# A gated delta rule and a soft mixture of experts on one core: 32-token chunks with the inverse on VectorE, against 64-token chunks with a block inverse on GpSimd and a list-scheduled order

## The chip, the core and the metric

One core of a Trainium2 chip runs the whole program. The number that counts is the device time of one launch in microseconds. PE is the matrix engine, DVE the vector engine, ACT the scalar engine, POOL is GpSimd, SP the queue that issues most transfers. All data are float32.

## What is computed

The first block is a delta rule over 768 tokens for 4 batches x 8 heads, head size 48; the second takes its output as 3072 rows of 384 and sends them through 32 slots of 8 experts.

```python
k_n = k / (norm(k) + 1e-06)
for t in range(S):                       # S = 768, for all 32 (b, h)
    kt, vt, bt = k_n[:, :, t], v[:, :, t], beta[:, :, t, None]
    y[:, :, t] = q[:, :, t] @ state
    v_old = state^T @ kt
    state = state + bt * outer(kt, vt - v_old)
x = y as (3072, 384)
logits = x @ phi                         # 32 slots
d = softmax over rows; slot_input = d.T @ x
slot_out[e] = relu(slot_input[e] @ w1[e]) @ w2[e]    # w1 384x1024, w2 1024x384, 8 experts
out = softmax over slots (logits) @ slot_out
```

The recurrence is worked in chunks. Within a chunk the tokens depend on each other through a unit lower triangular matrix (the products of the chunk's keys, scaled by beta). Its inverse T turns R = V - K S into the updates U; then S += K^T U and Y = Q S + (masked Q K^T) U.

## The kernel before

The token axis is cut into 24 chunks of C = 32. Partitions hold 4 head rows x 32 tokens; the 8 remaining (batch, head half) pairs, U = 8, lie along the free axis. A group is GC = 4 chunks, so there are NG = 6 groups.

- `load` (L80) brings k, q and v in, four transfers of 48 KB a chunk and tensor, in pieces of 192 bytes, from SP (the first q from ACT).
- `prep` transposes K and Q on PE (L173), evicts them on ACT (L176) and forms key-key and query-key products (L188), evicted by ACT into Lc (L194) and masked by DVE into AT (L195).
- `invert` works on one group. DVE transposes Lc in 32x32 blocks (L207), takes norms (L221 to L233), POOL scales the matrix by rows (L230, 128x1024), DVE eliminates in 31 steps of a multiply and a subtract each (L240, L243), POOL scales the result (L247) and DVE transposes it back into TT (L253). POOL also clears the next tt (L211).
- `chunk` is the step of the state: K S and Q S in one loop (L278), R on DVE (L283), T R (L289), U on ACT (L292), K^T U (L299), the state's two halves to SBUF by DVE and ACT (L309, L311), and the output (L316, L318). K S multiplies by a state of 96 columns whose off-diagonal halves are zero.
- `route` turns a group's outputs into logits, a running softmax over rows and the slots' sums (L336 to L418).
- The order is written out by hand. `prep` runs LEAD = 8 chunks ahead, loads AHEAD = 12. Between the parts of `chunk`, `fill()` puts in a share of the steps of `prep`, of a quarter of `invert` and of a quarter of `route`. Each engine executes its instructions in that order.
- After the loop the experts run. Two w1 (1.5 MB each) are loaded early, the other six and all eight w2 after the attention part's buffers are given back (L152, L156). Then `first` (L543 to L557), `second` (L567), and 24 output blocks (L593 to L600), one store each of 192 KB.

Of the kernel before, what the change touches and what calls it, by code (L numbers as in the profile page):

```python
# [1 line left out]

# [6 lines left out]
F32 = mybir.dt.float32  # L9
# [3 lines left out]
PSUM = bass.MemoryType.PSUM  # L13


@with_exitstack
def kernel(
# [11 lines left out]

# [3 lines left out]
    C = 32  # L44
    G = H // 4
    GC = 4
    NG = S // (GC * C)
    NCH = S // C
    U = B * G
    DP = 64  # L50
    GD = G * D
    E, Dm, F = moe_w1.shape
    NSL = moe_phi.shape[1]
    SPE = NSL // E
    NFC = F // P
    NKT = Dm // P
    assert G == 2 and B == 4 and GC * U == C and Dm == H * D and NSL == C

    cpool = ctx.enter_context(tc.tile_pool(name="const", bufs=1))
    wpool = ctx.enter_context(tc.tile_pool(name="wts", bufs=1))  # L60
    small = ctx.enter_context(tc.tile_pool(name="small", bufs=2))
    att = ExitStack()
    ps = att.enter_context(tc.tile_pool(name="ps", bufs=1, space=PSUM))
    io = att.enter_context(tc.tile_pool(name="io", bufs=2))
    wk = att.enter_context(tc.tile_pool(name="wk", bufs=2))
    psp = att.enter_context(tc.tile_pool(name="psp", bufs=1, space=PSUM))

    def pt(shape):
        return ps.tile(shape, F32, name="pt", tag="pt", bufs=2)


    LEAD, AHEAD = 8, 12
    NK, NQ = AHEAD + 1, AHEAD - LEAD + 1
    Ks = [io.tile([P, U, DP], F32, name=f"K{i}", bufs=1) for i in range(NK)]
    Qs = [io.tile([P, U, DP], F32, name=f"Q{i}", bufs=1) for i in range(NQ)]
    Vt = {}

    def load(src, dst, cc, eng):
        for h in range(4):
            eng.dma_start(  # L80
                out=dst[C * h:C * h + C, :, 0:D],
                in_=src.rearrange("b (g h) s d -> h s (b g) d", h=4)[h, cc * C:(cc + 1) * C])

    def load_k(cc, eng=nc.sync):
        load(k, Ks[cc % NK], cc, eng)

    def load_q(cc, eng=nc.sync):
        load(q, Qs[cc % NQ], cc, eng)

    def load_v(cc, eng=nc.sync):  # L90
        Vt[cc] = io.tile([P, U, D], F32, name="V", tag="V", bufs=7)
        load(v, Vt[cc], cc, eng)

    ident = cpool.tile([P, P], F32, name="ident")
    make_identity(nc, ident)
    for i in range(NK):
        nc.vector.memset(Ks[i][:, :, D:DP], 0.0)
        if i < NQ:
            nc.vector.memset(Qs[i][:, :, D:DP], 0.0)
    load_k(0)  # L100
    load_q(0, nc.scalar)
    load_k(1)
    load_q(1, nc.scalar)
    load_k(2)
    load_q(2)
    load_k(3)
    load_q(3)

    bb = cpool.tile([P, NG, C], F32, name="bb")
    for h in range(4):  # L110
        for c in range(GC):
            p0 = C * h + U * c
            nc.gpsimd.dma_start(
                out=bb[p0:p0 + U],
                in_=beta.rearrange("b (g h) (n c t) -> h c (b g) n t", h=4, c=GC, t=C)[h, c])
    phi = cpool.tile([GD, 4, NSL], F32, name="phi")
    for g in range(G):
        nc.gpsimd.dma_start(
            out=phi[g * D:(g + 1) * D],
            in_=moe_phi[g * 4 * D:(g + 1) * 4 * D].rearrange("(h d) s -> d h s", h=4))  # L120


    hm = cpool.tile([P, 4], F32, name="hm")
    nc.gpsimd.memset(hm, 1.0)
    nc.gpsimd.affine_select(out=hm, in_=hm, compare_op=ALU.is_ge, fill=0.0, base=0,
                            pattern=[[-C, 4]], channel_multiplier=1)
    nc.gpsimd.affine_select(out=hm, in_=hm, compare_op=ALU.is_ge, fill=0.0, base=C - 1,
                            pattern=[[C, 4]], channel_multiplier=-1)

    bdm = cpool.tile([P, 4, C], F32, name="bdm")  # L130
    nc.gpsimd.memset(bdm, 1.0)
    nc.gpsimd.affine_select(out=bdm, in_=bdm, compare_op=ALU.is_ge, fill=0.0, base=-1,
                            pattern=[[C, 4], [1, C]], channel_multiplier=-1)
    nc.vector.tensor_tensor(bdm, bdm, hm.unsqueeze(2).broadcast_to([P, 4, C]), op=ALU.mult)
    tri = cpool.tile([P, C], F32, name="tri")
    nc.vector.tensor_reduce(tri, bdm.rearrange("p h t -> p t h"), axis=AX.X, op=ALU.add)

    psS = psp.tile([P, 4, 512], F32, name="psS")
    St = []
    for i in range(2):  # L140
        t = wk.tile([P, 4, B, GD], F32, name=f"S{i}", bufs=1)
        nc.vector.memset(t, 0.0)
        St.append(t)


    NW1 = 2
    w1t, w2t = {}, {}


    def load_w1(e, pool, bufs):  # L150
        w1t[e] = pool.tile([P, NKT, F], F32, name="w1t", tag="w1t", bufs=bufs)
        nc.sync.dma_start(out=w1t[e], in_=moe_w1[e].rearrange("(p k) f -> p k f", k=NKT))  # L152

    def load_w2(e, pool, bufs):
        w2t[e] = pool.tile([P, NFC, Dm], F32, name="w2t", tag="w2t", bufs=bufs)
        nc.sync.dma_start(out=w2t[e], in_=moe_w2[e].rearrange("(p t) d -> p t d", t=NFC))  # L156

    KQ, AT, Lc, TT, nT = {}, {}, {}, {}, {}  # L160

    def prep(cc):

        n, c = divmod(cc, GC)

        def transposes(bh):
            if bh == 0:
                KQ[cc] = wk.tile([P, B, 2, P], F32, name="KQ", tag="KQ", bufs=LEAD + 1)
            tp = pt([P, 2, 2, P])
            for i in range(2):  # L170
                b = 2 * bh + i
                for a, src in enumerate((Ks[cc % NK], Qs[cc % NQ])):
                    nc.tensor.transpose(  # L173
                        tp[:, i, a, :],
                        src[:, b * G:(b + 1) * G, :].rearrange("p g d -> p (g d)"), ident)
            nc.scalar.activation(KQ[cc][:, 2 * bh:2 * bh + 2], tp, ACT.Copy)  # L176

        def products():
            AT[cc] = wk.tile([P, G, B, C], F32, name="AT", tag="AT", bufs=LEAD + 1)
            if c == 0:  # L180
                Lc[n] = wk.tile([P, C, C], F32, name="Lc", tag="Lc")
            pg = [pt([P, B, 2, C]) for _ in range(G)]
            for b in range(B):
                for h in range(4):
                    for g in range(G):
                        r = slice(DP * g, DP * g + D)
                        rh = slice(C * h, C * h + C)
                        nc.tensor.matmul(pg[g][rh, b], lhsT=KQ[cc][r, b, 0, rh],  # L188
                                         rhs=KQ[cc][r, b, :, rh],
                                         start=True, stop=True, skip_group_check=True)  # L190

            by = Lc[n].rearrange("p t (c b g) -> p c g b t", c=GC, b=B)
            for g in range(G):
                nc.scalar.activation(by[:, c, g], pg[g][:, :, 0, :], ACT.Copy)  # L194
                nc.vector.tensor_tensor(AT[cc][:, g], pg[g][:, :, 1, :],  # L195
                                        tri.unsqueeze(1).broadcast_to([P, B, C]), op=ALU.mult)

        return [lambda bh=bh: transposes(bh) for bh in range(2)] + [products]

    def invert(n):  # L200

        st = {}

        def spread():

            lb = st["lb"] = wk.tile([P, C, C], F32, name="lb", tag="lb", bufs=1)
            nc.vector.transpose(lb.rearrange("p t s -> p (t s)"),  # L207
                                Lc.pop(n).rearrange("p t c -> p (t c)"))
            tt = st["tt"] = wk.tile([P, C, C], F32, name="tt", tag="tt")
            ttf = tt.rearrange("p k i -> p (k i)")  # L210
            nc.gpsimd.memset(ttf, 0.0)  # L211
            nc.gpsimd.memset(ttf[:, 0:C * C:C + 1], 1.0)

        def norms():

            ssq = small.tile([P, C], F32, name="ssq", tag="ssq")
            nrm = small.tile([P, C], F32, name="nrm", tag="nrm")
            rn = small.tile([P, C], F32, name="rn", tag="rn")
            gm = st["gm"] = small.tile([P, C], F32, name="gm", tag="gm")
            dg = st["lb"].rearrange("p t s -> p (t s)")[:, 0:C * C:C + 1]  # L220
            nc.vector.tensor_scalar(ssq, dg, 1e-30, None, op0=ALU.max)  # L221
            nc.scalar.activation(nrm, ssq, ACT.Sqrt)
            nc.vector.reciprocal(rn, nrm)
            nc.vector.tensor_tensor(rn, rn, ssq, op=ALU.mult)
            nc.vector.tensor_tensor(nrm, nrm, rn, op=ALU.add)
            nc.vector.tensor_scalar(nrm, nrm, 0.5, 1e-6, op0=ALU.mult, op1=ALU.add)
# [402 lines left out]
```

## Time and profile before

| | us |
|---|---|
| median of 3 runs (lowest, highest) | 487.07 (486.02, 490.53) |
| span of the profiled execution | 489.7 |
| busy PE, DVE, ACT, POOL in it | 334.7, 245.1, 128.9, 63.6 |
| mean granted clock of PE | 0.729 |

Times in the profile's lines are microseconds, means of one instruction nanoseconds. A line names the engine, the line of the kernel, the operation, output and inputs, shapes, and a count. What stands behind `<-` released the instruction.

The timeline shows the same pattern in each group. The scaling by POOL (L230) stands at 142, 208, 273 and 338 us. The chunk loop ends at 424 us; w1 and w2 arrive from 400 to 461 us; the output goes out from 473 us.

### The profile page before, as it was taken

Reading aid. Unit: us, or ns where it says so; the run is one execution under the profiler, and the core shown is the slowest. Engines: PE = TensorE matmul, PEld = TensorE weight load, DVE = VectorE, ACT = ScalarE, POOL = GpSimd, SP = SyncE. Lnnn points to the kernel's source line nnn. Section 1 sums busy time; section 2 is a strip of 40 time slices with the busy share of each in tenths; the row PEclk is TensorE's granted clock in tenths of the full one; section 3 lists DMA queues with packets and bytes.
Section 4 is the critical chain, followed back from the end, with each engine's and each line's share of the span. In section 5 each row is a group of like instructions: output and inputs, shape, how many; then the busy total and the mean of one; then the engine's idle time right before and its main releaser. Section 6 shows DMA issues by size and latency. Waiting matters only on the chain.

```text
span 489.7 us, 20564 instructions
## 1 busy us (share of the span) xinstructions
PE 334.7 (68%) x9387; PEld 248.3 (51%) x9387; DVE 245.1 (50%) x679; ACT 128.9 (26%) x257; POOL 63.6 (13%) x88
## 2 busy tenths in 40 slices
PE   5743374656766758788677776876875865788586
PEld 4532263545645646666466655665664753532133
DVE  4159716972168942379721788325997212210033
ACT  2331122121322422332422233224312222111012
POOL 9210112012020040020210200202301000000000
PEclk9655556665766759755778577599798797799695
DMA  6557742320322213202221110010300029949427
GB/s 114 86 94 195 205 83 51 52 37 18 52 51 39 46 19 52 50 16 40 51 39 33 19 19 13 9 20 5 113 23 1 4 94 367 424 156 434 208 101 287
DMA packets 84759, 45.53 MB, mean 93 GB/s; under 512 B 79392, under 2 KB 82624, under 8 KB 82624
## 3 DMA queue, kind: packets, MB, share of 16 engines
q1 hardware_dynamic: 81920, 43.67, 32.4%
q8 instruction: 74, 1.21, 1.0%
q10 hardware_dynamic: 2176, 0.39, 0.4%
q0 software_dynamic: 576, 0.15, 0.3%
q14 instruction: 13, 0.11, 0.1%
HBM read 39.47 MB, written 4.72 MB: 90 GB/s over the span
## 4 chain that ended last, share of the span: by engine, by line
DVE 27%; issue 25%; PE 19%; SPq 10%; DMA 10%; POOL 5%; ACT 3%; DVEq 0%; POOLq 0%; ACTq 0%
DVE pr L240 9%; SPq L80 9%; DVE tt L243 9%; DMA w2t<-in_moe_w_dram 4%; PE pso L567 3%; DVE S L309 3%; PE psR L278 2%; PE pt L410 2%; DMA w1t<-in_moe_w_dram 2%; PE psY L278 2%; POOL lb L230 2%; DMA Q<-in_q_dram 2%; DVE TT L253 2%; PE ph L543 1%; DMA out_dram<-ob 1%
## 5 line engine op out<-in xcount | busy, mean ns | idle before, releaser
L240 DVE TENSOR_TENSOR pr<-tt,lb 128x31 f32<-128x31 f32 (+15 forms) x186 | 68.0, 365 | 17.7 <-POOL lb L230 12.2
L243 DVE TENSOR_TENSOR tt<-tt,pr 128x31 f32<-128x31 f32 (+15 forms) x186 | 66.3, 357 | 5.7
L289 PE MATMUL psW<-R,TT 32*32 32x48 f32 x1536 | 29.9, 242 | 47.0 <-DVE R L283 45.5
L173 PE MATMUL pt<-ident,K 128*128 128x128 f32 x96 | 36.0, 396 | 24.1 <-DVE AT L195 18.7
L289 PEld LDWEIGHTS psW<-R,TT 32*32 32x32 f32 x1536 | 25.7, 134 | 52.4 <-DVE R L283 49.3
L176 ACT ACTIVATE KQ<-pt 128x512 f32<-128x512 f32 x48 | 27.1, 595 | 73.9 <-PE pt L173 73.5
L278 PE MATMUL psR<-S,KQ 128*32 128x96 f32 x768 | 33.1, 324 | 17.7 <-DVE S L309 17.0
L316 PE MATMUL psY<-U,AT 32*32 32x48 f32 x1536 | 39.0, 256 | 3.2 <-issue 3.1
L195 DVE TENSOR_TENSOR AT<-pt,tri 128x128 f32<-128x128 f32 x48 | 11.9, 288 | 54.6 <-ACT Lc L194 54.4
L188 PE MATMUL pt<-KQ 48*32 48x64 f32 x1536 | 33.5, 246 | 6.2 <-ACT KQ L176 2.6
L309 DVE COPY S<-psS 48x768 f32<-48x768 f32 x23 | 22.1, 961 | 31.1 <-ACT S L311 30.7
L316 PEld LDWEIGHTS psY<-U,AT 32*32 32x32 f32 x1536 | 31.1, 143 | 9.2 <-issue 7.1
L299 PE MATMUL psS<-U,K 32*48 32x48 f32 x1472 | 25.3, 261 | 14.5 <-ACT U L292 11.6
L278 PEld LDWEIGHTS psR<-S,KQ 128*32 128x32 f32 x768 | 23.7, 145 | 22.4 <-DVE S L309 18.9
L188 PEld LDWEIGHTS pt<-KQ 48*32 48x32 f32 x1536 | 25.0, 119 | 16.0 <-ACT KQ L176 9.5
L173 PEld LDWEIGHTS pt<-ident,K 128*128 128x128 f32 x96 | 17.3, 186 | 30.7 <-DVE AT L195 20.2
L278 PE MATMUL psY<-S,KQ 128*32 128x96 f32 x768 | 32.3, 314 | 0.0
L292 ACT ACTIVATE U<-psW 128x384 f32<-128x384 f32 x24 | 11.8, 490 | 75.6 <-PE psW L289 75.6
L299 PEld LDWEIGHTS psS<-U,K 32*48 32x48 f32 x1472 | 20.4, 155 | 20.7 <-ACT U L292 15.7
L410 PE MATMUL pt<-Y,dr 32*32 32x97 f32 x768 | 25.1, 271 | 8.5 <-DVE AT L195 4.3
L230 POOL TENSOR_TENSOR lb<-lb,gm 128x1024 f32<-128x1024 f32 x6 | 11.5, 1911 | 141.0 <-DVE gm L229 141.0
L173 PE MATMUL pt<-ident,Q 128*128 128x128 f32 x96 | 29.7, 364 | 0.0
(124 smaller groups left out, 454.9 us busy)
## 6 DMA issues: line engine op xcount, KB each, us to landing
w1t<-in_moe_w_dram SPq DMA_DIRECT2D x8, 1536.0 KB, 8.2
w2t<-in_moe_w_dram SPq DMA_DIRECT2D x8, 1536.0 KB, 15.1
K<-in_k_dram SPq DMA_DIRECT2D x96, 48.0 KB, 2.3
V<-in_v_dram SPq DMA_DIRECT2D x96, 48.0 KB, 2.3
out_dram<-ob SPq DMA_DIRECT2D x24, 192.0 KB, 2.3
Q<-in_q_dram SPq DMA_DIRECT2D x88, 48.0 KB, 2.3
Q<-in_q_dram ACTq DMA_DIRECT2D x8, 48.0 KB, 3.0
bb<-in_beta_dram POOLq DMA_DIRECT2D x16, 6.0 KB, 3.0
```

The source lines that it names most:

```text
L80: eng.dma_start(out=dst[C * h:C * h + C, :, 0:D], in_=src.rearrange("b (g h) s d -> h s (b g) d", h=4)[h, cc * C:(cc + 1) * C])
L173: nc.tensor.transpose(tp[:, i, a, :], src[:, b * G:(b + 1) * G, :].rearrange("p g d -> p (g d)"), ident)
L176: nc.scalar.activation(KQ[cc][:, 2 * bh:2 * bh + 2], tp, ACT.Copy)
L188: nc.tensor.matmul(pg[g][rh, b], lhsT=KQ[cc][r, b, 0, rh], rhs=KQ[cc][r, b, :, rh], start=True, stop=True, skip_group_check=True)
L240: nc.vector.tensor_tensor(prv, tt[:, j, 0:m].unsqueeze(1).broadcast_to([P, w, m]), lb[:, j, j + 1:C].unsqueeze(2).broadcast_to([P, w, m]), ...
L243: nc.vector.tensor_tensor(tt[:, j + 1:C, 0:m], tt[:, j + 1:C, 0:m], prv, op=ALU.subtract)
L278: nc.tensor.matmul(dst[hs[h], b].rearrange("p g d -> p (g d)"), lhsT=kq[:, b, a, hs[h]], rhs=old[:, h, b, :], start=(b == 0), stop=False, ...
L289: nc.tensor.matmul(pw[hs[h], u], lhsT=T[hs[h], u], rhs=R[hs[h], u], start=(u == 0), stop=True, skip_group_check=True)
L299: nc.tensor.matmul(psS[DP * g:DP * g + D, h, b * D:(b + 1) * D], lhsT=K[hs[h], b * G + g, 0:D], rhs=Ut[hs[h], b * G + g], start=(cc == 0 a ...
L309: nc.vector.tensor_copy(dst, src)
L316: nc.tensor.matmul(py[hs[h], b, g], lhsT=at[hs[h], g, b], rhs=Ut[hs[h], b * G + g], start=False, stop=True, skip_group_check=True)
L410: nc.tensor.matmul(pa[r], lhsT=st["dr"][r, c, b, :], rhs=Yn[r, c, b, 0:GD + 1], start=(b == 0), stop=(b == B - 1), skip_group_check=True)
```

## The change

It is a new kernel. Only the launch code and the mathematics are the same.

**Layout.** Chunks have C = 64 tokens; there are 12 of them, worked in 6 pairs. Partitions hold 2 batch halves x 64 tokens, and the 16 (batch, head) combinations of each half, U = 16, lie along the free axis. One chunk of k, q or v is two transfers of 64 partitions (192 KB each).

**Keys.** Each key is scaled once by sqrt(beta)/(norm + 1e-6), and V by sqrt(beta), so that the triangular matrix comes out symmetrically scaled and needs no scaling of its rows afterwards. The square roots and the reciprocals are powers on POOL.

```diff
+        pl.op(f"sq{c}", "ACT", act(UD), ... ACT.Square)
+        pl.op(f"ssq{c}", "DVE", dve(UD), ... tensor_reduce(m[:, 0], s, op=ALU.add))
+            nc.gpsimd.tensor_tensor(m[:, 1], m[:, 0], half[:, 0:1].broadcast_to([P, U]), op=ALU.pow)
+            nc.gpsimd.tensor_scalar(m[:, 1], m[:, 1], 1e-6, None, op0=ALU.add)
+            nc.gpsimd.tensor_tensor(m[:, 2], m[:, 1], half[:, 1:2].broadcast_to([P, U]), op=ALU.pow)
+            nc.gpsimd.tensor_tensor(m[:, 2], m[:, 2], sbt[:, c], op=ALU.mult)
+        pl.op(f"ks{c}", "DVE", ... u3(K(c)) = u3(K(c)) * m[:, 2].unsqueeze(2) ...)
+        pl.op(f"vs{c}", "DVE", ... u3(V(c)) = u3(V(c)) * sbt[:, c].unsqueeze(2) ...)
```

K and Q are transposed by plain matmuls with a stationary operand of 48 columns (`turn`), 16 for each tensor and chunk.

**Inverse.** `invert` treats a pair of chunks: the 64x64 triangle of each head has four diagonal blocks of 16, and 15 steps eliminate all of them at once, on DVE for the first pair and on POOL for the other five. Where before one step worked on up to 256 columns, a step now works on at most 128 in two strided halves.

```diff
+        eng = "DVE" if n == 0 else "POOL"
+        api = nc.vector if n == 0 else nc.gpsimd
+        pl.op(f"lb{n}", "DVE", 1.2, lambda e: nc.vector.transpose(lb, AN(n) ...))
+        pl.op(f"tt{n}", "POOL", 1.1, f, ...)          # memset tt, ones on the diagonal
+        for j in range(15):
+            m, w = j + 1, 15 - j
+                api.tensor_tensor(prv, tv[:, :, j, 0:m].unsqueeze(2).broadcast_to([P, 2, w, m]),
+                    lv[:, :, j, j + 1:16].unsqueeze(3).broadcast_to([P, 2, w, m]), op=ALU.mult)
+                api.tensor_tensor(tv[:, :, j + 1:16, 0:m], tv[:, :, j + 1:16, 0:m], prv,
+                                  op=ALU.subtract)
+        pl.op(f"dn{n}", "DVE", 1.2, ... nc.vector.transpose(DN(n), tt))
+        pl.op(f"dt{n}", "DVE", 1.2, ... nc.vector.transpose(DT(n), tt))
```

`couple` builds the 64-token inverse from the 16-token ones on PE: five products a chunk (named pp, px, pz, p6, p2; 64, 65, 32, 64 and 32 matmuls) with an eviction behind each. Rings of one buffer (LB, TT, DT, DN) tie one pair's inverse to the next.

**State.** `chain` keeps the state as 48x48 blocks for each head (no zero halves), accumulates it on DVE, and needs for a chunk: 32 matmuls K S, R on DVE (128x768), 64 matmuls T R, U on ACT (128x768), 32 matmuls K^T U, and S + that on DVE (128x768). The output `au` and its two evictions hang beside it.

```diff
+            pl.op(f"ks_{c}", "PE", ..., writes=[("pch", 3 * c, 0)], lat=0.25)
+            pl.op(f"r{c}", "DVE", dve(UD), ... ujg(Rt(c)) = ujg(V(c)) - pv ...)
+        pl.op(f"tr{c}", "PE", 0.75, f, reads=rk + [("XT", c, 0), ("XT", c, 1)], ...)
+        pl.op(f"u{c}", "ACT", act(UD), ...)
+            pl.op(f"ku{c}", "PE", 0.4, f, reads=[("K", c, "sc"), ("U", c, 0)], ...)
+                    nc.vector.tensor_tensor(new, old, pv, op=ALU.add)
```

**Order.** The body no longer issues instructions directly. It hands `Plan` about a thousand operations with an engine (or a choice of ACT and DVE for evictions), an estimated duration, what they read and write, and rings of buffers. `Plan.simulate` walks through them in time, gives each free engine the ready operation of highest priority, keeps six rotating PSUM banks, and repeats this for 12 rounds with priorities from the round before; the best round's order is then issued, engine by engine, with a dependency that holds each engine to it.

```diff
+                for o in ready[e]:
+                    if best is not None and prio[o.i] <= prio[best.i]:
+                        continue
+                        if o.ps and sum(1 for b in o.ps if b not in held) > len(banks):
+                            continue
+                        if o.lazy and late:
+                            continue
+                    best = o
...
+    sched = pl.run()
+    for o in sched:
+        o.fn(o.on)
+                tc.add_manual_dep(ins, prev, DependencyInfo(NoSync, DATA), reason="order")
```

**Experts.** w1 comes in 48 pieces of 128x512 and w2 in 64 pieces of 128x384, all from SP, into buffers of the attention part as these come free; four pieces of w1 have a place of their own. The last 20 w2 pieces take the places of the first w1 pieces.

```diff
+        pl.op(f"dma w1.{e}.{kk}.{f}", "SP", 0.68, ... dma_start(out=t, in_=w1src[e, :, kk, HF*f:HF*f+HF]),
+            free=keys, lazy=True)
+        pl.op(f"dma w2.{e}.{t}", "SP", 0.52, ... dma_start(out=x, in_=w2src[e, :, t]), free=keys, lazy=True)
...
+                    for x in range(2):
+                        nc.sync.dma_start(out=oap[x, i % 2, C * c:C * c + C], in_=ob[64 * x:64 * x + 64])
```

The 24 output blocks go out as 48 stores of 96 KB, and each is scaled by the row's softmax sum as it is evicted.

In counts, from the two programs:

| | before | after |
|---|---|---|
| matmuls in the program | 4856 | 7549 |
| DVE instructions | 679 | 268 |
| ACT operations without table loads and transfers | 248 | 198 |
| POOL compute instructions | 70 | 227 |
| transfers of k, q, v | 288 | 72 |
| transfers of weights | 16 | 112 |
| stores | 24 | 48 |

## The prediction

> **What bounds the kernel now.** I read the page from the top (busy shares, slices, the chain that ended last), then PE's waits, the timeline of a few groups, and windows of the last 100 us.
>
> ```profile
> PE 334.7 (68%) x9387; PEld 248.3 (51%) x9387; DVE 245.1 (50%) x679; ACT 128.9 (26%) x257; POOL 63.6 (13%) x88
> PEclk9655556665766759755778577599798797799695
> DVE 27%; issue 25%; PE 19%; SPq 10%; DMA 10%; POOL 5%; ACT 3%; DVEq 0%; POOLq 0%; ACTq 0%
> L240 DVE TENSOR_TENSOR pr<-tt,lb 128x31 f32<-128x31 f32 (+15 forms) x186 | 68.0, 365 | 17.7 <-POOL lb L230 12.2
> L243 DVE TENSOR_TENSOR tt<-tt,pr 128x31 f32<-128x31 f32 (+15 forms) x186 | 66.3, 357 | 5.7
> ```
>
> No engine is full. DVE heads the chain, and 134.3 of its 245.1 us are the 372 elimination steps (L240, L243), 22.4 us in series for each of six groups. PE's 68% is partly slow matmuls: the clock row is mostly 0.5 to 0.8.
>
> ```profile
> PE psW L289 <- DVE R L283: 45.5, 15, 10.1
> PE pt L173 <- DVE AT L195: 18.7, 6, 8.9
> PE psR L278 <- DVE S L309: 17.0, 10, 3.4
> ```
>
> PE waits up to 10.1 us for R, which stands behind elimination steps on DVE's in-order queue. Group follows group at 65.6 us (207.70 to 273.34 in the chain). The loop ends at 424 us; the last 65 are experts, weights and output.
>
> **What goes.** DVE's elimination (134.3 us), the products with half-empty states (L278, 59.5), half of the chunks, and three of four transfers for q, k, v. I sum per engine, then by stages.
>
> **PE.** The trace must be read with care: its 9387 records belong to 4856 matmuls, as L289 shows (24 x 32 = 768 in the program, 1536 recorded). A plain float32 matmul leaves two records, a transpose one. The new order holds 7549 matmuls, 106 of them transposes, so some 14990 records, 60% more than before. One group at both clocks:
>
> ```profile
> 238.33 1.48 PE L289 MATMUL psW<-R,TT 32*32 32x48 f32 x64 [2.03 <-DVE R L283]
> ...
> 392.05 0.88 PE L289 MATMUL psW<-R,TT 32*32 32x48 f32 x64
> 392.75 0.66 PE L410 MATMUL pt<-Y,dr 32*32 32x97 f32 x18
> ```
>
> The second (clock 1.00) is followed after 0.70 us: 10.9 ns a record. The first (clock 0.53) needs about twice that. At 1.00, 32 records of L278 (96 columns, four side by side) go by in 0.68 us, 21.3 ns each, so one place of the array takes 4 x 21.3/96 = 0.89 ns a column; 64-column records of L188 need 17 ns, a transpose 107. I take 0.89 x columns / matmuls side by side, and 10.9 at least. All 12 chunks at full clock:
>
> - K and Q turned by plain matmuls: 768 records of 128 columns, two side by side, 57 ns: 44 us
> - key and query products: 1536 of 64 columns at 17, 768 of 32 at 10.9: 35
> - coupling: 4608 at 10.9, 1536 of 32 columns in pairs at 14.2, 24 of 512 columns at 456: 83
> - state chain: 1408 at 10.9, T R 1536 of 48 columns in pairs at 21.3: 48
> - output: 1408 at 10.9, 768 at 21.3: 32
> - routing: 90 transposes, 144 records of 128 and 48 of 384 columns in fours: 18
>
> Together 260 us, or 21.7 a chunk. The same prices on the 8870 attention records of before give 170 us, 19 ns each on average. So PE's work grows by half. In the new code T R is entered with 0.75 us, where these prices give 2.7; the order was made for a PE twice as fast.
>
> [...] The trace has 10.9, and the sum goes by that.
>
> **DVE.** Rows: 128x384 from PSUM 0.546, S 768 columns 0.961, eviction of 512 0.692 (L557), two SBUF inputs 0.16 + 1.05 ns a column. So 24 masks x 0.68 = 16; 12 sums of squares x 0.95 = 11; 24 scalings of K and V x 0.96 = 23; 22 R and S x 0.95 = 21; 30 evictions x 0.69 = 21; 18 transposes x 1.92 (L253) = 35; routing 14; the first pair's elimination 30 x 0.2 + 2720 x 1.05 ns = 9; the rest 10. Sum 160 us, 13 a chunk, under PE. ACT: 96 x 0.595 + 24 x 0.80 + 20 x 0.49 + 16 = 102 us, under it too; table loads fall from nine (11.5 us) to one.
>
> **POOL.** Its three sizes (128: 0.406, 384: 0.854, 1024: 1.911) lie on 0.2 us + 1.7 ns a column. A pair's elimination is 30 x 0.2 + 2720 x 1.7 ns = 10.6 us. No row shows the power operation: 0.2 like any other, or ten times that, 2 us (24 of them, +43 in all, +5 on the start). I take 0.25, next to POOL's small rows. Loop for a pair: memset 1.1, elimination 10.6, norms 2, two DVE transposes with their queue about 5: 19 us under PE's 43.
>
> POOL and DVE also hold each other up:
>
> ```profile
> 372.00 1.91 POOL L247 TENSOR_TENSOR tt<-tt,gm 128x1024 f32<-128x1024 f32 x1 [19.22 <-DVE tt L243]
> 372.64 1.42 DVE L358 TENSOR_TENSOR el<-lg,mx 128x128 f32<-128x128 f32 x1
> ```
>
> el takes 0.29 elsewhere; here it ends as POOL does. R, with one operand in PSUM, doesn't stretch. 24 scalings with two SBUF operands will each wait for one short step: at most 10 us on DVE, hidden by PE's 260.
>
> **State chain** of a chunk: 0.9 + R 0.95 + T R 2.9 + U 0.80 + 0.9 + S 0.95 + hand-overs 0.5 = 7.9 us, also under 21.7. So PE sets the pace from its first scaled key: K landed 5.6 (first matmul of before 5.36), table load 1.28, square 0.80, sum 0.95, norms 1, scaling 0.96, so 11 us (16 with norms at their upper bound).
>
> What share p of these prices PE reaches decides. Before, p was 170/424 = 0.40 in the loop, and 0.57 in its best 30-us windows (892 records from 180 to 210 us, 903 from 330 to 360, x 19 ns / 30). They hold waits for DVE that the new one hasn't, since DVE and ACT have 9 and 13 us to spare a chunk. What stays are hand-overs, waits marked "issue" of 0.7 to 1.7 us in fast stretches, and clock drops: the clock is 1.00 until 238, then 0.53 behind a gap of 2.03 us. In series at half clock PE recovers (208 to 218 us). I take p = 0.8, the middle between the best windows of before and 1: 260/0.8 = 325, and the loop ends at 11 + 325 = 336.
>
> [...] The row shows a drop behind 2.03 us.
>
> **Tail.** On SP's queue the weights stand behind the loads, in the order in which buffers come free; the w1 pieces in the last chunk's KQ have 47 w2 pieces queued behind them: 4 x 256 + 47 x 192 KB = 10.3 MB after the loop.
>
> ```profile
> 415.00:425.00 10.00, 7.61 (x170) 6.67 (x170) 2.43 (x14) 1.11 (x3) 0.84 (x4) 0.61 1.00 424
> 475.00:480.00 5.00, 4.46 (x15) 3.07 (x16) 2.23 (x4) 2.44 (x5) 0.00 (x0) 0.73 1.03 366
> ```
>
> At 366 GB/s (last column; 1.5-KB rows, as most new pieces have) that is 28 us, beside routing and merging (9), L543's part (96 x 127 ns = 12) and most of L567's (128 x 87 ns = 11). PE is done at +34; sum, scaling and first block 4. The 24 stores become 48, and SP issues one each 0.5 us now: 24 us and 2.3 to land. Tail 64; 48 if the stores go at the rate of the data (13 us) and weights at 424 GB/s; 70 with gaps.
>
> Sum: 11 + 325 + 64 = 400 of span, against 489.7; the median of before is 487.07, 0.5% under its span, so 398.
>
> **Rivals.** First, slower: PE's stalls and clock drops stay as in the best windows of before. At p = 0.57, 260/0.57 = 456 and the kernel takes 531. From p = 260/(487 - 75) = 0.63 down it is slower than before. For it: no 30-us window of before is better, and the order is made for a PE twice as fast. The 64-row tiles (state, output) are in no row either, and were they a third dearer, p would have to be higher by as much. Against: the large waits of PE came from DVE.
> Second, PE runs dense at p = 0.95 or more: 11 + 274 + 50 = 335. For it: six PSUM banks and independent work between the steps of the chain. Against: "issue" waits grow with the count of records.
> Third, POOL's strided steps and powers cost far more than its rows. It decides from 43 us a pair, (43 - 8)/38 = 0.9 us an operation; at 2 us a pair takes 84, and 43 + 5.5 x 84 + 64 = 569. Against: POOL's small rows are 0.1 to 0.4 us.
>
> **How the numbers follow.** p from 0.7 to 0.95, 349 to 446 us, has 0.58. The second rival and what lies below 349, 0.10. 446 to 482, 0.09. The first rival, slower, 0.17; the third 0.03; the same within 1% (what a run of this kernel can tell) 0.03. 336 to 490 takes in the first case, two thirds of the second, the third and the nearest of the rest, about 0.78; the likeliest case alone is 349 to 446. Faster 0.77, same 0.03, slower 0.20.
>
> **What would show it.** About 15000 PE records, PE busy above 85% from 45 us on, at a clock of 0.85 to 1; few waits over 1 us; DVE near 170 us, POOL near 70 with steps of 0.2 to 0.5; stores 0.5 us apart. Wrong if small groups need other than 11 to 14 ns a record, if POOL or DVE heads the chain, or if PE idles with the clock at 0.5.

## The result

The changed kernel takes 758.21 us (median of five runs, 753.67 to 766.26) against 487.07 us (484.09 to 490.53): 1.552 times as long, 95% interval 1.541 to 1.563. Slower by 271 us, where a time of 398 us was forecast. The profiled execution, with a span of 764.5 us, is the slowest of the five, 1.1% above their median; the interval goes by the other four.

The lines of the new page that answer to those of before: busy shares, granted clock, the instruction queue, the chain of work that ended last.

```profile
PE 550.9 (72%) x14992; PEld 439.5 (57%) x14992; DVE 175.1 (23%) x268; ACT 105.1 (14%) x205; POOL 174.6 (23%) x227
...
PEclk9998565576657565555555555555556555577755
...
q8 instruction: 117, 1.92, 1.0%
...
PE 69%; DVE 9%; ACT 8%; issue 6%; POOL 6%; DMA 0%; DVEq 0%; SPq 0%; ACTq 0%
```

The bound has moved where the forecast put it: DVE fell from 27% to 9% of the chain, PE heads it with 69%. But PE's busy time is 551 us and its clock is mostly at half. (The nines at the left are no measurement: the trace's first clock record comes at 58 us, and the K turn needs 104 ns a record before it, twice its full-clock price.)

The start, on POOL's timeline (start, duration, instruction, what the idle time before it waited for):

```profile
8.16 30.96 POOL L403 TENSOR_TENSOR sbt<-sbt,half 128x192 f32<-128x192 f32 x1 [3.72 <-DVE sbt L400]
39.10 2.90 POOL L432 TENSOR_TENSOR NRM<-NRM,half 128x16 f32<-128x16 f32 x1
42.09 0.26 POOL L433 TENSOR_SCALAR NRM<-NRM 128x16 f32<-128x16 f32 x1
42.43 2.92 POOL L434 TENSOR_TENSOR NRM<-NRM,half 128x16 f32<-128x16 f32 x1
```

The power of 192 columns takes 31 us, 161 ns a column; those of 16 columns 2.9 us each. The addition of the same 16 columns takes 0.26. PE's first K turn (a product that transposes K) follows at 46.7 us.

The loop (first K turn to last output product) and the tail, as windows. The columns are the stretch, its length, busy time and instructions of PE, PEld, DVE, ACT and POOL, then the mean clock, the DMA share and GB/s:

```profile
46.70:655.70 609.00, 480.00 (x14594) 412.49 (x14594) 143.13 (x204) 96.31 (x187) 134.04 (x204) 0.58 0.17 44
655.70:764.50 108.80, 67.76 (x352) 24.15 (x350) 25.49 (x55) 5.81 (x15) 0.00 (x0) 0.63 0.44 131
```

Stage by stage: start 46.7 us (forecast 11), loop 609.0 (325), tail 108.8 (64). The misses are 36, 284 and 45 us, together the 364.5 between 764.5 and the forecast span of 400, and 78% of them lie in the loop. There PE is busy for 79% at a clock of 0.58.

### The profile page after: what moved, and what is told of

Read it like the earlier page. It is cut to its first block, busy times and chain, and to the rows that moved or that the text cites. A ratio compares the mean times of both kernels' runs of the same rounds, so it can differ in the third digit from the quotient of the medians.

```text
span 764.5 us, 31290 instructions
## 1 busy us (share of the span) xinstructions
PE 550.9 (72%) x14992; PEld 439.5 (57%) x14992; DVE 175.1 (23%) x268; ACT 105.1 (14%) x205; POOL 174.6 (23%) x227
## 4 chain that ended last, share of the span: by engine, by line
PE 69%; DVE 9%; ACT 8%; issue 6%; POOL 6%; DMA 0%; DVEq 0%; SPq 0%; ACTq 0%
PE rot L331 52%; PE pch L331 13%; POOL sbt L403 4%; PE rot L726 3%; ACT KQ L321 2%; DVE AT L499 1%; DVE K L326 1%; ACT XT L321 1%; ACT AN L321 1%; DVE KQ L324 1%; ACT O L321 1%; POOL NRM L434 1%; POOL NRM L432 1%; ACT NP L321 1%; DVE AN L324 1%
## 5 line engine op out<-in xcount | busy, mean ns | idle before, releaser
L331 PE MATMUL rot<-ident,K 128*48 128x128 f32 x384 | 39.7, 385 | 49.0 <-DVE K L438 41.6
L331 PE MATMUL pch<-R,XT 32*64 32x48 f32 (+1 forms) x1408 | 70.1, 290 | 0.7 <-ACT XT L321 0.7
L331 PEld LDWEIGHTS pch<-R,XT 32*64 32x64 f32 (+1 forms) x1408 | 67.0, 192 | 4.1 <-issue 1.9
L331 PE MATMUL rot<-KQ 48*32 48x64 f32 (+2 forms) x2304 | 46.1, 266 | 23.2 <-issue 8.4
L432 POOL TENSOR_TENSOR NRM<-NRM,half 128x16 f32<-128x16 f32 x12 | 34.8, 2897 | 122.6 <-DVE NRM L427 122.6
L331 PEld LDWEIGHTS rot<-KQ 48*32 48x32 f32 (+1 forms) x2304 | 40.7, 154 | 29.5 <-issue 10.8
L331 PE MATMUL rot<-DN,AN 16*32 16x16 f32 (+1 forms) x2304 | 42.4, 208 | 19.7 <-issue 9.0
L331 PE MATMUL rot<-ident,Q 128*48 128x128 f32 x384 | 41.9, 394 | 13.2 <-DVE AN L324 3.6
L331 PE MATMUL rot<-U,AT 64*64 64x48 f32 x776 | 42.3, 292 | 0.7 <-ACT KQ L321 0.7
L331 PEld LDWEIGHTS rot<-U,AT 64*64 64x64 f32 x776 | 39.3, 206 | 2.7 <-ACT KQ L321 1.0
L434 POOL TENSOR_TENSOR NRM<-NRM,half 128x16 f32<-128x16 f32 x12 | 35.1, 2922 | 1.0
```

The costliest lines, as they stand in the source:

```text
L331: nc.tensor.matmul(o, lhsT=l, rhs=r, start=st, stop=sp, skip_group_check=True)
L432: nc.gpsimd.tensor_tensor(m[:, 1], m[:, 0], half[:, 0:1].broadcast_to([P, U]), op=ALU.pow)
L434: nc.gpsimd.tensor_tensor(m[:, 2], m[:, 1], half[:, 1:2].broadcast_to([P, U]), op=ALU.pow)
```

## The experiments

Three theories at first. A: the form of the small tiles keeps the clock at half. B: gaps between the groups do, since the order was made for a faster PE. C: PE's instructions arrive at a fixed rate. Beside them the powers at the start.

**Streams of one form (m1).** Each form of the new kernel alone, no waits inside: one such loop for each form, whose tiles take turns. (The idle stretches came out at about 1 us instead of 8, so a stream began at the clock that the one before had left.)

```
for i in range(n):
    r0, r, c, p0, m = forms[i % len(forms)]
    ...
    nc.tensor.matmul(ps[p0:p0 + c, ..., 0:m], lhsT=Y[r0:r0 + r, a:a + c], rhs=rh,
                     start=True, stop=True, skip_group_check=True)
```

> Nothing of the reference is computed (the output is zeros): eleven streams of one form of float32 matmul each, with no wait inside; each stream is issued once behind an idle stretch of some 8 us (about 20 us of work at half clock), then nine 128x512 products on the whole array, then the same stream again. Theory A (the form decides): the streams with 16 to 64 rows, whose weights have as many columns as the moving operand or more (16x32 with 16 columns, 32x32 with 16, 32x64 and 64x64 with 48, 48x64 with 48), stay at a granted clock of 0.5 although PE never waits, and fall from 1.0 back to 0.5 within 3.4 to 7 us behind the whole-array products; 128x48 with 128 columns and the whole-array products rise to 1.0. Theory B (gaps decide): every stream rises to 1.0 after 3.4 to 7 us of unbroken work and stays there in its second half; then the half clock of the changed kernel comes from waits of 1 to 3 us between groups. Either way the stream shows what a record costs at each clock: 53 ns for 32x64 with 48 columns at 0.5, some 27 to 29 at 1.0. Beside it: a square root of 128x16 on ACT, which should take 0.2 to 0.3 us, where the power on POOL took 2.9.

The timeline of PE in the stream of 32x16 tiles with 16 columns (start, duration, records, idle before):

```profile
162.98 1.24 PE L70 MATMUL ps_w32x16n<-Y_w32x16n 32*16 32x16 f32 x128 [2.00 <-issue]
166.44 1.25 PE L70 MATMUL ps_w32x16n<-Y_w32x16n 32*16 32x16 f32 x128 [2.21 <-issue]
169.89 1.25 PE L70 MATMUL ps_w32x16n<-Y_w32x16n 32*16 32x16 f32 x128 [2.20 <-issue]
173.62 1.25 PE L70 MATMUL ps_w32x16n<-Y_w32x16n 32*16 32x16 f32 x128 [2.48 <-issue]
```

Exactly 128 records (with their weight loads 256 instructions) run in 1.25 us, then PE waits for nothing that the program shows. The instruction queue of the same stretch, 159 to 176 us:

```profile
GB/s 0 0 0 39 0 0 0 0 0 0 0 0 39 0 0 0 0 0 0 0 39 0 0 0 0 0 0 0 39 0 0 0 0 0 0 0 39 0 0 0
...
q8 instruction: 5, 0.08, 1.9%
```

Five packets of 16 KB, one for each block of 128 records; the blocks start 3.45 to 3.73 us apart. So theory C holds for such streams: 8.3 ns a record inside a block, 27.6 ns over 2352 records. The form of the row that the forecast took 10.9 ns from (32x32, 48 columns, four side by side) shows 10.6 ns inside a block at full clock and 26.0 over its 1000 records.

Theory A, from streams that no block boundary broke (windows as above):

```profile
109.00:128.00 19.00, 18.86 (x703) 18.76 (x701) 14.35 (x3) 0.00 (x0) 0.00 (x0) 0.50 0.02 5
300.00:319.00 19.00, 19.00 (x362) 19.00 (x361) 0.00 (x0) 0.00 (x0) 0.00 (x0) 0.50 0.01 3
348.00:367.00 19.00, 19.00 (x482) 19.00 (x480) 0.00 (x0) 0.00 (x0) 0.00 (x0) 0.50 0.01 3
```

32x32 with 16 columns, T R's 32x64 with 48 and its 32x32 with 48, all in pairs: busy for the whole 19 us (18.86 in the first), clock 0.50 to the end. The 64x64 pair, at the same 53 ns a record, rose 3.6 us after its start and went to 29.2. So B alone doesn't explain the clock, since work without a gap isn't enough, and A was too wide: the 64x64 pair too has more weight columns than moving ones (64 and 48). Tiles of 48 rows (48x64 with 48 moving columns, four in turns) ran unbroken at 0.50 for 11.5 and 12.8 us. ACT's square root of 16 columns took 0.215 us.

**The powers (e1).** A square root on ACT, and on DVE addition, reciprocal and product:

```diff
-            nc.gpsimd.tensor_tensor(m[:, 1], m[:, 0], half[:, 0:1].broadcast_to([P, U]), op=ALU.pow)
...
+        pl.op(f"nq{c}", "ACT", 0.25, lambda e: nc.scalar.activation(m[:, 1], m[:, 0], ACT.Sqrt),
...
+            nc.vector.reciprocal(m[:, 2], m[:, 1])
```

> The powers on POOL are replaced by a square root on ACT and an addition, a reciprocal and a product on DVE. If the power of 192 columns (30.97 us) and the first two of 16 (5.8) lie on the path of the start, PE's first scaled turn begins near 12 us instead of 46.7 and the kernel is 33 to 38 us shorter: 720 to 726. If PE's later work is held by something else (rival: the loads or the order), the gain is below 15 us. A granted clock of 0.58 to 0.65 and PE busy at 0.75 to 0.82 in the loop stay either way.

725.9 us (721.5 to 729.0), ratio to before 1.491 (1.478 to 1.503). The first K turn begins at 12.0 us instead of 46.7, and 32.3 of these 34.7 us arrive at the end. The loop is 597.4 us, 2% shorter, about what runs of one kernel differ by, with PE busy for 474.5: the rest of the loss is still there. What follows is built on this kernel, unless it says otherwise.

**The order (e2, e3).** In the changed kernel, PE's durations in the plan replaced by traced ones; alone, and with the norms.

```diff
+    PE_US = {"pa": 2.2, "pq": 1.7, "pp": 1.7, "px": 3.1, "pz": 1.7, "p6": 3.4, "p2": 1.7,
+             "ks_": 1.7, "tr": 5.9, "ku": 1.3, "au": 5.7, "xt": 0.9, ...
```

> Only the PE durations that the order is made with are changed, to what the trace showed at half clock (T R 5.9 us for 0.75, output 5.7 for 1.0, turns 1.67 for 0.46 and so on). Theory A (form decides the clock): PE's idle share in the loop falls from about 0.2 to 0.1, the clock stays at 0.55 to 0.65, and the time falls by 30 to 70 us, 690 to 730. Theory B (gaps decide the clock): with fewer and shorter gaps the clock rises above 0.75 and the time falls below 620. If the order has nothing to do with it, the time stays within 2%.

> Both edits together. If they are independent, the gains add: 33 to 38 us of the start and what the order gives, 650 to 695 by theory A, below 590 by theory B.

798.5 us (796.6 to 802.7), 40 slower than the changed kernel, and 740.6 us (735.6 to 743.8), 15 slower than e1. The loop of e2 is 628 us, PE's busy time there 483, the clock 0.57 from the first clock record on. The new order moved evictions from ACT (56 us busy for 105) to DVE (230 for 175). That the order was made for a PE twice as fast is true; correcting it gave no gain, and since the evictions moved with it, what the order alone costs isn't shown.

**More dense work (e4).** Three 128x512 products in bfloat16, in front of eight groups a chunk.

```diff
+            nc.tensor.matmul(o, lhsT=wb[:, 0:P], rhs=wb, start=True, stop=True,
+                             skip_group_check=True)
```

> On top of e1_norms, three bfloat16 products of 128x128 with 512 columns, whose result is overwritten, go in front of eight of the groups of each chunk (key and query products, the six coupling groups but one, output): 288 records more, 61 us of PE's time at full clock and 123 at half. Theory A (the clock rises only where many rows of the array stream, not for want of gaps): the granted clock of the loop rises above 0.8, a record of T R's first half goes from 53 to about 29 ns, and the kernel gets faster in spite of the added work, 560 to 640 us. Theory B (hand-overs and gaps hold the clock): the clock stays below 0.65 and the kernel takes 790 to 850. Theory C (PE is fed with instructions at a fixed rate, 16 KB or 128 records in 3.4 us): even with the clock up, the loop doesn't fall below 119 x 3.4 = 405 us.

784.3 us (766.0 to 786.5). Neither forecast: the clock in the loop rose from 0.58 to 0.65, far from 0.8, and the loop of the profiled execution got 63 us longer; even the fastest run is 40 us behind e1. The granted clock is switched in steps of 3.41 us (every stretch but the last in the clock records of the kernel before and of the changed one is a multiple of it, 45 and 35 of them), and the bursts last 1.3 us or less: that they were too short is argued, not shown.

**Fewer records (e5, e6, e7).** Products read the upper halves of their operands, as bfloat16 numbers with fewer digits: first the coupling's, then all of attention's.

```diff
+    def hi(x):
+        return x.bitcast(BF16)[..., 1::2]
+
+    def mh(o, l, r, st=True, sp=True):
+        mm(o, hi(l), hi(r), st, sp)
```

> On top of e1_norms, the coupling products read the upper 16 bits of their float32 operands as bfloat16 (truncated): one record and one pass instead of two records, 3084 records less, 93 blocks of instructions instead of 117. Theory C: the loop is fed 24 x 3.4 = 82 us faster; theory A alone: the coupling groups shrink from some 11.7 us a chunk at half clock to about 4, at most 90 us. Together 60 to 110 us: 615 to 665. Rival (hand-overs between PE and DVE or ACT set the pace): less than 25 us, over 700.

> As e5, but for all products of prep, coupling and chain; routing and experts stay float32. Some 7800 records in 62 blocks, 55 x 3.4 = 187 us less to feed, and a quarter of the streaming. Theories A and C: 200 to 320 us less than e1_norms, 410 to 525. If hand-overs set the pace: over 600.

622.4 us (606.7 to 630.2) and 441.7 us (439.9 to 443.8; ratio to before 0.907, 0.900 to 0.914). e6 lies within what A and C expected, and so does e5's median; its fastest run gained more than they said. With hand-overs as the pace they would be over 700 and 600. e6's loop is 319 us, at T R's half-clock price all through (26.6 ns, half of 53.3).

Passes (what a record costs PE: 26.6 ns for T R's at half clock, 53.3 in float32) and records (7408 in the loop, 14593 in e1) fell together there. To part them, each of e6's products is issued twice, once with zeros:

```diff
-        mm(o, hi(l), hi(r), st, sp)
+        mm(o, hi(l), zb[a:a + h.shape[0], 0:h.shape[-1]], st, False)
+        mm(o, hi(l), h, False, sp)
```

> As e6_half_all, but each of those products is issued twice, once with a moving operand of zeros and once with its own, added up in PSUM: the records of the float32 kernel again (some 14600, 115 blocks of instructions) at one pass each. Theory C (feeding of instructions is a bound of its own): a loop of at least 113 x 3.4 = 385 us, 470 us in all at the least, 130 us or more of the 280 us between e6 and e1 come back, 570 to 680. Theory A (what the passes cost at half clock is all): each record costs half of the float32 one, so no group takes longer than in e1 and the time lies near the middle or below, 500 to 570.

620.8 us (619.8 to 623.2), in the range of C and above that of A alone. Its loop beside e6's, one window each:

```profile
12.50:511.00 498.50, 303.94 (x14581) 259.67 (x14593) 143.89 (x232) 107.95 (x207) 63.49 (x160) 0.78 0.25 59
```

```profile
12.50:331.60 319.10, 178.64 (x7408) 143.27 (x7413) 143.11 (x232) 106.07 (x203) 66.44 (x160) 1.00 0.37 88
```

(The clocks there are again mostly unrecorded.) Same DVE, ACT and POOL work, 114 blocks of instructions instead of 58: 179 us more. That doesn't part the two cleanly, since the second product takes PE's time as well: PE was busy for 125 us more. But PE idles 39% of e7's loop, and its waits marked "issue", for nothing that the profile shows, grew from 15.6 to 88.0 us. Those of e6, then of e7 (total, times, longest):

```profile
PE rot L339 <- issue: 13.9, 14, 3.3
PE pch L339 <- issue: 1.7, 2, 1.1
```

```profile
PE rot L347 <- issue: 77.7, 67, 3.6
PE pch L347 <- issue: 10.3, 9, 2.2
```

So the supply costs time of its own once the passes are cheap. From e1 (597 us, the same 114 blocks) to e7 are 99 us for the passes.

Is e6's gain one of the design? The same reading in the kernel before (b1):

```diff
-                                         lhsT=KQ[cc][r, b, 0, rh],
+                                         lhsT=hi(KQ[cc][r, b, 0, rh]),
```

> The kernel before with the same reading of the upper halves in its key, state, T R and output products (3944 of its 4856 matmuls or so; its transposes stay as they are). If PE's records were its bound as in the new kernel, it gains in proportion, 100 us or more, below 390. If DVE's elimination sets its pace, as its chain of waits said, it gains less than 60 us: 430 to 480, and the gain of e6 over before isn't one of the number format alone.

444.4 us (444.0 to 445.4), ratio 0.905 (0.899 to 0.911), as much as e6. DVE still heads its chain with 32%. So the number format is worth about 45 us there, and the new design with it is no better than the old one with it.

**Rows and the clock (m2).** The loop of m1 with 128 moving columns.

> Nothing of the reference is computed (zeros as output): eleven unbroken streams of one form with 128 moving columns, long enough per record that the feeding of instructions cannot break them (53 ns a record or more at half clock), each behind an idle stretch of 8 us, then the whole-array products, then the form again. Theory A in its finer form (the share of the array's rows that stream decides): forms on one or two of the four row groups (32 rows once, twice; 32x64 twice; 32x128 once; 64 rows once) stay at 0.5 for all of their 22 us and fall back within 10 us from 1.0; forms on all four (32x32 four times, 32x64 four times, 64x64 twice, 128x32 four times) rise within 3.4 to 7 us and stay; 48-row pairs (96 rows) and 16-row quadruples (64 rows) lie between. If the share of the whole array decides instead, 32x128 once and 32x64 twice (a quarter) behave as 32x32 four times (a quarter). If only unbroken work counts, all rise.

Three windows: 32x32 twice, 32x64 twice, 32x128 once, all with 128 columns:

```profile
71.00:91.00 20.00, 20.00 (x192) 16.74 (x190) 15.82 (x3) 0.00 (x0) 0.00 (x0) 0.50 0.00 1
181.00:201.00 20.00, 20.00 (x192) 20.00 (x190) 0.00 (x0) 0.00 (x0) 0.00 (x0) 0.50 0.01 2
258.00:277.00 19.00, 19.00 (x92) 19.00 (x92) 0.00 (x0) 0.00 (x0) 0.00 (x0) 0.50 0.00 1
```

One or two row groups (of 32 rows each) stayed at half in these three for 19 and 20 us; 64x64 rose after 5.7 us. From full clock one row group fell back, two held it for their 11.5 us, against the expectation; in m1 T R's pair, with 48 columns, fell back after 5.3. Most other streams began at full clock, so their rise was left to the last run.

**T R on four row groups (e8, e9), and its forms alone (m3).** Its two halves in turns, on e1 and on e6.

```diff
+            for u in range(8):
+                first(8 + u)
+                second(u)
```

> On top of e1_norms, only the order within T R: the products of the first halves of eight heads (row groups 0 and 2, bank 1) alternate with those of the second halves of the other eight (row groups 1 and 3, bank 0), so that the middle half of T R streams through all four row groups. At half clock T R should go from 64 x 53 + 64 x 40 ns = 5.9 us to 32 x 53 + 32 x 53 (with the other 32 beside them) + 32 x 40 = 4.7 us or less, 12 to 15 us in all, and 10 to 25 us with what the clock gains: 700 to 716. If T R is covered by other work or limited by the feeding of instructions: less than 5 us.

> The same order of T R on top of e6_half_all: T R is 32 x 26.6 + 32 x 19.6 ns = 1.5 us there at half clock, so at most 4 us in 12 chunks: 436 to 442, within what three rounds can tell.

751.4 us (747.4 to 755.7) and 454.0 us (452.4 to 455.3): 25 and 12 us slower, or 21 and 9 by their ratios to the kernel before. T R in the changed kernel and in e8:

```profile
226.00 6.35 PE L331 MATMUL pch<-R,XT 32*64 32x48 f32 x128
```

```profile
199.94 8.50 PE L331 MATMUL pch<-R,XT 32*64 32x48 f32 x128
```

2.15 us more in a group, 26 us in twelve: what PE gets more to do here is paid nearly in full. (In e9 a group takes 3.41 us for 1.79, 19 us in twelve, and about half of it shows.) Why it was dearer, streams of these forms show:

> Nothing of the reference is computed (zeros as output). Streams as in m2_rows, this time each behind an idle stretch that waits for the stream before (8 us of DVE work in between). First, T R's two forms with 48 moving columns (32x64 on row groups 0 and 2, 32x32 on 1 and 3): in turns of two, of eight and of thirty-two, beside 32x64 alone and 32x32 alone on all four row groups. If a change of the tile's form stops PE (theory), turns of two need 80 to 85 ns a record at half clock as in e8, turns of eight about 60, turns of thirty-two about 48, and the forms alone on four row groups 27 and 20. If it is the overlap of row groups over the same columns (rival), 32x64 alone on four row groups is as slow as turns of two. Second, the clock: 32x32 on four row groups with 128 columns, the pair of 48 rows and the 128x32 quadruple, all unbroken, now start from 0.5: by the share of rows they rise to 1.0 within 3.4 to 7 us; if it takes more than that, they stay at 0.5.

At half clock a record took 85.0 ns in turns of two, 56.2 in turns of eight, 49.7 in turns of thirty-two. 32x64 alone on four row groups took 26.7, and 32x32 alone 20.0, both before a block boundary broke them: half of what their pairs on two row groups took in m1 (53.3 and 40.0). So row groups over the same columns did run side by side. Without overlap between the forms a record would take 46.6 ns (the mean of 53.3 and 40.0 of the pairs in m1); a turn of two, eight or thirty-two products holds 4, 16 or 64 records, so by that estimate each change of form cost about 150, 150 and 200 ns more. And the clock, at the start of the 32x32 quadruple and of the 48-row pair, before and after it switched:

```profile
311.00:316.00 5.00, 5.00 (x100) 5.00 (x96) 0.00 (x0) 0.00 (x0) 0.00 (x0) 0.50 0.01 3
318.00:323.00 5.00, 5.00 (x192) 5.00 (x188) 0.00 (x0) 0.00 (x0) 0.00 (x0) 1.00 0.03 7
349.00:353.00 4.00, 4.00 (x41) 4.00 (x39) 0.00 (x0) 0.00 (x0) 0.00 (x0) 0.50 0.02 4
355.00:361.00 6.00, 6.00 (x114) 6.00 (x112) 0.00 (x0) 0.00 (x0) 0.00 (x0) 1.00 0.01 3
```

With 128 moving columns, forms on all row groups rose after 4.9 to 6.2 us of unbroken work, and 32x64 with 48 on four row groups after 5.7; turns on two row groups at a time stayed at half for 26 us. The 48-row tiles of m1 with 48 moving columns did not rise in 12.8 us, so the row groups alone don't decide, and what does stays open.

## Why the prediction was wrong

The step that failed is "I take p = 0.8". PE reached 260/609 = 0.43 of the price list's speed, hardly more than the 0.40 of before, and below the 0.57 that the first rival took. No run shows the 0.95 behind the 349 us at which the likeliest case began; it was the author's estimate. In terms of the sum: the work was 277 us at full clock (480.0 us busy at 0.577, an estimate, since ends of matmuls are modelled) where 260 stood; the clock added 203 us, and PE's idle time 129, where p = 0.8 left 65 for both. Of the idle time 30.9 us are waits marked "issue", and the other 98 us hand-overs from ACT and DVE, at most 2.6 us each. Two readings stood behind it.

- **The price of a record.** "10.9 ns a record" is right inside a block of 128 and was used as a lasting rate. With 14594 records the loop has 114 blocks, and at 3.4 us each (m1's blocks started 3.45 us apart at the closest) they need 388 us by an estimate even if nothing else held PE, more than the 325 forecast. At half clock this floor was not the pace: a block took 5.3 us, and its waits marked "issue" are the 30.9 us (rows below). The page of before showed the supply: the waits marked "issue" were read as stalls that "grow with the count of records", without asking what they wait for. Before has 74 blocks, which need 252 of its 490 us.

```profile
PE rot L331 <- issue: 24.9, 22, 2.3
PE pch L331 <- issue: 6.0, 5, 1.9
```

- **The clock.** It is the larger of the two. It was to rise once PE no longer waited for DVE. It fell, from 0.70 in the loop of before (from its first clock record) to 0.58. Pairs on two of four row groups (T R and four of the coupling's products) didn't raise it even unbroken: T R's two forms and the coupling's 32x32 with 16 columns stayed at 0.50 for 19 us in m1. The forms that did took 3.6 to 6.2 us of unbroken work; that the kernel's groups of them end or are broken too soon (the output's 64x64 products run for 3.4 us at half clock, 64 records of 53.1 ns) is argued, not shown. "A drop behind 2.03 us" was read from one gap.

PE's work itself was near, 277 against 260. Single prices: the products of K and U 11.6 ns at full clock (10.9 said), the 64x64 pair 29.2 (21.3 said), T R's first half 53.3 at half clock where 21.3 said 42.6: a tile with more weight columns than moving ones cost its weight columns.

- **Start**, 11 us said, 46.7 measured. The third rival had the power's price, but as 2 us an operation and as a pace of the loop. It goes by columns (161 to 183 ns each), and 31 of its us stand ahead of everything. e1: 32 us.
- **Tail**, 64 said, 108.8 measured. Routing and merging took 20.3 us (9 said), experts and sum 39.5, the stores 49 (26 said). The last term was priced by SP's issues alone, but most of the 24 blocks go one after the other, 2.35 us a step: PE 1.64 at half clock, then the copy that PE waits for. Two of them on PE's timeline:

```profile
734.82 1.64 PE L331 MATMUL rot<-so,cT 32*128 32x384 f32 x2 [0.71 <-DVE K L326]
737.18 1.64 PE L331 MATMUL rot<-so,cT 32*128 32x384 f32 x2 [0.71 <-DVE K L326]
```

- **Right**: 14992 records (14990 said), DVE 175 us (160), ACT 105 (102), a pair's elimination on POOL 11.9 us (59.4 in five pairs; 10.6 said), DVE off the head of the chain. POOL did not slow the loop: with POOL's work cut from 174.6 to 64.8 us (e1) its length stayed within 2%.
- **The first rival** had the sign and the place, PE's stalls and clock, but in the size it was far off too (531). Of its reasons, the output's 64-row tiles were indeed more than a third dearer, the order is not shown (e2), and the supply of instructions is in none of them.

What a full clock alone would gain stays open: no run held it up without adding work. With the tail as it is, no order of these float32 records can beat the kernel before, by an estimate from the runs: start 12, 114 blocks at 3.4 us and tail 109 make 509 us.

## What to carry to other kernels

Count a kernel's instructions before its flops: many small matmuls can be paid by their number, and a duration read from one short burst is not a rate that lasts (8.3 ns a record inside a block of m1, 27.6 over 2352 records). Before a clock is forecast, ask which rows of the array the new tiles fill and whether their forms alternate (19 us of T R's pairs stayed at 0.50; turns of two took 85 ns a record). An operation that no row shows needs a price per element (the power took 161 to 183 ns a column), and the widest use of it ahead of the first dependent work is where it hurts.

## What the runs showed of the hardware

- PE's instructions came in packets of 16 KB, one for 128 records and their weight loads: 117 in the changed kernel, at least 3.29 us apart (at half clock), and 74 in the kernel before, at least 3.38 us apart (at full clock). In m1's stream the blocks started 3.45 to 3.73 us apart.
- The granted clock changed in steps of 3.41 us, between 0.5 and 1.0, in the kernel before and in the changed one. It rose within 3.6 to 6.2 us of unbroken work on 64x64 pairs (m1, m2), on 48-row pairs with 128 moving columns and on four row groups of 32 (m3). It did not rise on one or two row groups of 32 in 19 to 26 us (m1, m2, m3), nor on 48x64 tiles with 48 moving columns in 12.8 us (m1).
- A change of the tile's form between 32x64 and 32x32 in turns of two made a record cost 85 ns at half clock (m3), where each form alone took 20 to 53 (m1, m3).
- In m1's pairs a record cost its moving columns or its weight columns, whichever were more: 53.3 ns for 64 weight columns and 48 moving, 40.0 for 32 and 48, 26.8 for 32 and 16, all at half clock.
- The power on POOL took 161 to 183 ns a column, ACT's square root of 192 columns 0.36 us in all (m1).
